# Block 1 of the first sequence: normed by ScalarE, GpSimd and a DMA transpose instead of by matmuls

## The chip, the cores and the metric

The kernel runs on one core of a Trainium2 chip, in one launch. The metric is device time in microseconds (us). The core has five engines, each with its own instruction queue: TensorE (PE, matmuls; its weight loads are shown apart as PEld), VectorE (DVE), ScalarE (ACT), GpSimd (POOL) and SyncE (SP, which only issues DMAs). Matmuls write to PSUM, from where ACT or DVE must copy results to SBUF.

## The reference

Eight sequences of 3008 tokens with 256 channels are mixed along time by a learned filter in the frequency domain, and every token then goes through a gated feed-forward layer of width 1536.

```
X = rfft(x, axis=1);  y = irfft(X * (filt_r + 1j * filt_i), n=3008, axis=1)
t = y.reshape(8 * 3008, 256)
xn = t / sqrt(mean(t * t, axis=-1) + 1e-6) * rms_g
out = (silu(xn @ w_gate) * (xn @ w_val)) @ w_out
```

Inputs and output are float32.

## The kernel before, in words

**The transform.** 3008 = 47 x 64, so the transforms are done in two steps each by matmuls with constant tables. The A-step (`a_unit`, psum tile `psa`) goes over the 64 part, its result is stored to a DRAM scratch `z_tmp` (`z_store`) and read back in another order (`t2_load`); the B-step (`b_unit`, `psb`) goes over the 47 part, and DVE and GpSimd multiply by the filter; DMA transposes (`yt_load`) turn the product; the inverse B-step (`bi_unit`, `psi`) collects in `uu`; four DMA transposes (`t4_load`, tiles `t4`) turn that; the last inverse step is the psum tile `psn` of the norm steps. The first sequence has its own faster variants, written out ahead of the main loop.

**The items.** The feed-forward part of a sequence is cut into 6 blocks (m) of 4 x 128 tokens. A block goes through 12 column groups (jt) of the hidden layer. An item is one (sequence b, block m, group jt): `gv` does four matmuls into `pg` and `pv` (L546; weights `wg` and `wv`, moving operand `xn`), a Silu on ACT (L550) and a product on DVE (L551, tile `hh`); `down`, two items later, does four matmuls with `hh` into `po` (L563). There are 8 x 6 x 12 = 576 items, in that order. So `xn` of block m of sequence 0 is first read by item 12 m.

**What is placed between the items.** Everything else is put into slots by a planner: `at(slot, fn, ...)` appends a step to the plan of an item, and the step is issued between that item's `gv` and its `down`. `fit(slot, need...)` moves a step on to the next slot where the resources that it needs are free: psum bank M (number 0), psum bank B (number 3), and ACT and DVE, whose loads in slots are summed and compared with a room per slot. What is planned first takes its slots first. Steps in the list `late` (`q_unit` alone) come behind `down`.

**How a block is normed.** The usual way (`norm_plan`) has these steps:

- `n_unit`, twice: one matmul of 128x512 into `psn` (L314), copied to the float32 tile `y` by ACT (L195)
- `sq_unit`, twice, an item later: ACT squares two token groups of 256 channels each and sums along the channels (L322, `junk`, sums in `ss`)
- `stat_unit`: GpSimd makes `rho` = (ss / 256 + eps)^-0.5 (L330, L332)
- `xt_unit`: GpSimd multiplies `y` by `rho` into the float16 tile `xt` (L340)
- `tr_unit`: SyncE issues a DMA transpose from `xt` to `xn` (L349), since the matmuls of `gv` need channels on partitions

Block 0 of sequence 0 is done ahead of the loop by `first_norm`. Block 1 of sequence 0 has a way of its own, in which the transform gives `y` already turned, so that no DMA is in it:

- `n_first` in slot 3: eight matmuls of 128x128 (L483) into two psum banks, ACT squares both (L486, `sq`) and copies both to `y`
- `q_unit` in slot 5: eight matmuls of one column with a vector of ones (L497, `psq`) sum the squares; DVE scales (L501), GpSimd takes the power (L503)
- `scale_split` in slot 7: DVE splits `rho` into two float16 parts `hl` (L509, L510)
- `scale_apply` in slot 9: eight matmuls of 128x128 (L519, `psr`) spread `hl` over the partitions, and DVE multiplies (L524) into `xn`

**Queues.** Each engine runs its instructions in the order in which they are issued. SyncE's queue holds the `t4` transposes, the z stores and loads, the xn and yt transposes and the output stores (L581). GpSimd issues the loads of x (`x_load`, L186, 384 KB each, float32 to float16) between its own computations; an x load of the next sequence but one can go once the A-step has read the tile that it overwrites (`xp` has four buffers). Around the change, the first thirteen items of the loop also hold the A-steps 2 to 11 of sequence 1, their four z stores, and the x loads of sequence 2:

```
at(s, a_unit, b, i, e, 0 if k == 'M' else 3)
if i % 3 == 2:
    at(s + 1, z_store, b, i // 3)
    if b + 1 < B:
        at(max(s + 2, XAT.get(b + 1, (0,) * 4)[i // 3]), x_load, b + 1, i // 3)
```

Of the kernel before, what the change touches and what calls it, by code (L numbers as in the profile page):

```python
# [10 lines left out]
FP32 = mybir.dt.float32  # L11
FP16 = mybir.dt.float16
AXT = mybir.ActivationFunctionType
ALU = mybir.AluOpType
# [6 lines left out]
P = 128  # L21
D = 256
B = 8
# [9 lines left out]
Y_SCALE = N * S_INV_B * S_INV_A  # L33
XC = 6
# [67 lines left out]
def kernel(  # L102
# [11 lines left out]
    nc = tc.nc  # L114
# [17 lines left out]
    xtp = ctx.enter_context(tc.tile_pool(name="xtp", bufs=2))  # L132
    up = ctx.enter_context(tc.tile_pool(name="up", bufs=2))
    xnp = ctx.enter_context(tc.tile_pool(name="xnp", bufs=4))
    hp = ctx.enter_context(tc.tile_pool(name="hp", bufs=4))
    op = ctx.enter_context(tc.tile_pool(name="op", bufs=2))
# [4 lines left out]
    psB = ctx.enter_context(tc.tile_pool(name="psB", bufs=1, space=bass.MemoryType.PSUM))  # L141

    tab = glob.tile([P, 5 * P], FP16)
    wa, wai, ident = (tab[:, ts(i, P)] for i in range(3))
# [13 lines left out]
    ones = glob.tile([P, 1], FP16)  # L158
    epsb = glob.tile([P, 1], FP32)
    warm = glob.tile([P, 4], FP32)  # L160
    mhalf = glob.tile([P, 4], FP32)
    seen = glob.tile([P, 4], FP16)

    st = {b: {"x": {}, "t1": {}, "t2": {}, "s": {}, "yt": {}, "t4": {}, "y": {}, "sq": {},
              "u": {}, "xn": {}} for b in range(B)}
# [4 lines left out]
    def y_tile():  # L170
        t = stg.tile([P, 2, 4, 256], FP32, tag="stg", name="y")
        return t.rearrange("p a b c -> p (a b c)")[:, 0:1024].rearrange("p (a e) -> p a e", a=2)
# [16 lines left out]
    def bank(i, name):  # L189
        pool, tag = ((psM, "mx"), (psG, "pg"), (psV, "pv"), (psB, "mb"), (psO, "po0"))[i]  # L190
        return pool.tile([P, 512], FP32, tag=tag, name=name)

    def copy(eng, out, in_, scale=None):
        if eng == "A":
            nc.scalar.activation(out=out, in_=in_, func=AXT.Copy, **({} if scale is None else {"scale": scale}))  # L195
        elif scale is None:
            nc.vector.tensor_copy(out=out, in_=in_)
        else:
            nc.vector.tensor_scalar(out=out, in0=in_, scalar1=scale, scalar2=None, op0=ALU.mult)
# [271 lines left out]
        fill(3)  # L471
        st[0]["xn"][0] = xn

    def n_first(m):
        y = y_tile()
        sq = xtp.tile([P, 4, D], FP16, tag="xt", name="sq").rearrange("p (a e) d -> p a (e d)", a=2)
        psn = [bank((0, 3)[h], "psn") for h in range(2)]
        for h in range(2):
            for q in (2 * h, 2 * h + 1):
                n1p = 4 * m + q  # L480
                src = st[0]["t4"][n1p // XC][:, n1p % XC]
                for dh in range(2):
                    nc.tensor.matmul(psn[h][:, ts(2 * (q % 2) + dh, P)], src[:, ds(dh * P, P)], wai,  # L483
                                     start=True, stop=True)
        for h in range(2):
            nc.scalar.activation(out=sq[:, h, :], in_=psn[h], func=AXT.Square)  # L486
        for h in range(2):
            copy("A", y[:, h, :], psn[h])
        st[0]["sq"][m] = sq
        st[0]["y"][m] = y  # L490

    def q_unit(m):
        sq = st[0]["sq"].pop(m)
        ps = psB.tile([P, 4], FP32, tag="mb", name="psq")
        for q in range(4):
            for dh in range(2):
                nc.tensor.matmul(ps[:, q:q + 1], sq[:, q // 2, ts(2 * (q % 2) + dh, P)], ones,  # L497
                                 start=(dh == 0), stop=(dh == 1))
        u = up.tile([P, 4], FP32, tag="u", name="u")
        rho = up.tile([P, 4], FP32, tag="rho", name="rho")  # L500
        nc.vector.tensor_scalar(out=u, in0=ps, scalar1=1.0 / D, scalar2=1e-6 * Y_SCALE * Y_SCALE,  # L501
                                op0=ALU.mult, op1=ALU.add)
        nc.gpsimd.tensor_tensor(out=rho, in0=u, in1=mhalf, op=ALU.pow)  # L503
        st[0]["u"][m] = rho

    def scale_split(m):
        rho = st[0]["u"].pop(m)
        hl = up.tile([P, 2, 4], FP16, tag="hl", name="hl")
        nc.vector.tensor_copy(out=hl[:, 0, :], in_=rho)  # L509
        nc.vector.tensor_tensor(out=hl[:, 1, :], in0=rho, in1=hl[:, 0, :], op=ALU.subtract)  # L510
        st[0]["u"][m] = hl

    def scale_apply(m, bk):
        hl = st[0]["u"].pop(m)
        y = st[0]["y"].pop(m)
        ps = bank(bk, "psr")
        for q in range(4):
            for e in range(2):
                nc.tensor.matmul(ps[:, ts(q, P)], hl[:, e, q:q + 1].to_broadcast([P, P]), ident,  # L519
                                 start=(e == 0), stop=(e == 1))  # L520
        xn = xnp.tile([P, 4, 2, P], FP16, tag="xn", name="xn")
        pv = ps.rearrange("p (q t) -> p q t", q=4)
        for h in range(2):
            nc.vector.tensor_tensor(out=xn[:, 2 * h:2 * h + 2],  # L524
                                    in0=pv[:, 2 * h:2 * h + 2].unsqueeze(2).to_broadcast([P, 2, 2, P]),
                                    in1=y[:, h, :].rearrange("p (q e t) -> p q e t", q=2, e=2), op=ALU.mult)
        st[0]["xn"][m] = xn

    SPLIT = ((0, 0, 0), (B - 1, 5, JT - 1))
    hh_of = {}  # L530
    po_of = {}
# [78 lines left out]
    with tc.manual_schedule():  # L610
# [48 lines left out]
        todo = [(i, f, dh) for i in range(2) for f in range(2) for dh in range(2)][:7] + [(2, 0, 0)]  # L659
# [56 lines left out]
        first_norm()  # L716

        items = [(b, m, jt) for b in range(B) for m in range(6) for jt in range(JT)]
        plan, late = {}, {}
        front = (sq_unit, s_part, add_unit)  # L720
        load = {r: [0.0] * (len(items) + 99) for r in "MBAV"}
        room = {"A": 0.8, "V": 0.7}
# [2 lines left out]
            load["V"][i] = 0.68  # L725

        def at(slot, fn, *a):
            todo = (late if fn == q_unit else plan).setdefault(slot, [])
            if fn in front:
                todo.insert(0, (fn, a))  # L730
            else:
                todo.append((fn, a))

        def fit(slot, *need, keep=True):
            def fits(r, d, cost):
                i = slot + d
                if r in "MB":
                    return load[r][i] == 0
                wait = 0.0
                for k in range(max(0, i - 16), i + 16):  # L740
                    wait = max(0.0, wait + load[r][k] + (cost if k == i else 0.0) - room[r] - 0.15 * (k < 72))
                    if k >= i and wait > 0.6:
                        return False
                return True

            while not all(fits(*n) for n in need):
                slot += 1
            if keep:
                for r, d, cost in need:
                    load[r][slot + d] += cost  # L750
            return slot

        def norm_plan(b, m, slots, r):
            for i in range(2):
                s = fit(slots[i], ("M", 0, 1), ("A", 0, 0.6), ("A", 1, 0.82))
                at(s, n_unit, b, m, i)
                at(s + 1, sq_unit, b, m, i)
            for d, fn in zip(r, (stat_unit, xt_unit, tr_unit)):
                at(s + d, fn, b, m)
            assert s + r[-1] + 1 < 72 * b + 12 * m  # L760
# [18 lines left out]
        def b_plan(b, slots, lags, soft=()):  # L779
# [18 lines left out]
                        at(last, bi_unit, b, u)  # L798
            return last

        at(3, n_first, 1)
        at(5, q_unit, 1)
        at(7, scale_split, 1)
        at(9, scale_apply, 1, 3)
        load["M"][3] = load["M"][4] = 1
        load["B"][3] = load["B"][4] = load["B"][5] = load["B"][9] = load["B"][10] = 1
        load["A"][3] = load["A"][4] = 1.2
        for m, n_at in ((2, 12), (3, 20), (4, 31), (5, 42)):
            norm_plan(0, m, (n_at, n_at + 2), (2, 3, 6))
        for b in range(1, B):  # L810
            t = (b - 1) * 72
# [31 lines left out]
        early = {}  # L843
# [11 lines left out]
        for i in range(len(items) + 4):  # L855
            for fn, a in early.pop(i, ()):
                fn(*a)
            if i < len(items):
                gv(*items[i])
            for fn, a in plan.pop(i, ()):  # L860
                fn(*a)
            if 2 <= i < len(items) + 2:
                b, m, jt = items[i - 2]
                if jt == 1 and i > JT:
                    down(b, m, 0)
                if jt or i < JT:
                    down(b, m, jt)
                if items[i - 2][2] == JT - 1:
                    stores[i + 1] = items[i - 2][:2]
            for fn, a in late.pop(i, ()):  # L870
                fn(*a)
            if i in stores:
                o_store(*stores[i])
        assert not plan and not late and not early


# [28 lines left out]
```

## Time and profile before

| what | value |
|---|---|
| median of 3 runs | 860.96 us (860.88 to 861.07) |
| the profiled execution's own time | 861.07 us |
| its span, first to last instruction | 859.3 us |
| mean granted TensorE clock | 0.999 |
| busy: PE, PEld | 849.6, 532.8 us |
| busy: DVE, ACT, POOL | 557.2, 612.7, 298.1 us |
| items 0 to 12 start | 43.5 to 61.83 us from the span's start |

The profile is of one execution. Its times count from the first instruction, so they are set against the span, and 1.8 us of the 861.07 lie around it. Busy time is that of an engine's own instructions; matmuls are pipelined, and a matmul's recorded duration is longer than the distance to the next one's start. A timeline row gives the start, the time from the first start to the last end, the engine, the line, the operation with its tiles and the count, and in brackets the idle time before it and what ended that. A DMA's row is only its issue; its landing is in the DMA view, whose packet counts are given by queue: q0 is GpSimd's, q1 SyncE's.

### The profile page before, as it was taken

The page shows a single profiled execution, that of the slowest core. Times are in us where ns is not written, and L with a number is a line of the kernel's source. Part 1 is how long each engine was busy: PE and PEld are TensorE (multiplying, and loading weights), DVE is VectorE, ACT ScalarE, POOL GpSimd, SP SyncE. Part 2 cuts the span into 40 slices and gives each one's busy share as a digit, 9 for nine tenths or more (in the row PEclk, how much of TensorE's full clock was granted, in tenths as well). Part 3 has the DMA queues.
Part 4 walks back from the last instruction along what each step waited for, and adds up shares of the span by engine and source line. Part 5 has one row for each costly group of instructions (what it writes and reads, how often), then busy time and mean ns, then how long its engine had stood idle before and what let it go on. Part 6 is the DMA issues. An engine that isn't in the chain of part 4 may idle for free.

```text
span 859.3 us, 17024 instructions
## 1 busy us (share of the span) xinstructions
PE 849.6 (99%) x6142; PEld 532.8 (62%) x6142; DVE 557.2 (65%) x926; ACT 612.7 (71%) x1339; POOL 298.1 (35%) x346
## 2 busy tenths in 40 slices
PE   8999999999999999999999999999999999999997
PEld 6756666666666666666666666666666666665664
DVE  5857755776666666666666676767666665555554
ACT  4987787787687757887578865887567765777443
POOL 5724832443154412543044430444123430132000
PEclk9999999999999999999999999999999999999999
DMA  9996777755976466756745658434564331521101
GB/s 284 269 202 128 154 157 178 148 123 132 187 137 144 104 145 111 161 117 129 150 121 118 119 107 185 105 81 114 128 118 93 98 72 41 127 49 50 63 25 50
DMA packets 198237, 107.98 MB, mean 126 GB/s; under 512 B 158566, under 2 KB 182520, under 8 KB 198152
## 3 DMA queue, kind: packets, MB, share of 16 engines
q1 hardware_dynamic: 189464, 85.52, 44.4%
q0 software_dynamic: 8544, 21.24, 12.8%
q8 instruction: 48, 0.79, 0.4%
q14 instruction: 37, 0.30, 0.1%
q10 hardware_dynamic: 144, 0.13, 0.0%
HBM read 45.78 MB, written 35.65 MB: 95 GB/s over the span
## 4 chain that ended last, share of the span: by engine, by line
PE 97%; DMA 1%; ACT 1%; DVE 0%; POOL 0%; issue 0%; POOLq 0%
PE po L563 29%; PE pv L546 28%; PE pg L546 28%; PE psb L241 3%; PE psi L285 3%; PE psn L314 2%; PE psa L206 2%; DMA fs<-in_filt_i_dram 1%; PE psy L418 1%; PE psf L389 1%; PE pst L367 0%; POOL xc L186 0%; DVE s L231 0%; ACT ff L195 0%; ACT L470 0%
## 5 line engine op out<-in xcount | busy, mean ns | idle before, releaser
L551 DVE TENSOR_TENSOR hh<-pv,sg 128x512 f16<-128x512 f32 (+2 forms) x578 | 391.8, 678 | 284.1 <-ACT sg L550 222.6
L550 ACT ACTIVATE sg<-pg 128x512 f16<-128x512 f32 (+2 forms) x578 | 337.6, 584 | 215.4 <-PE pg L546 211.5
L546 PE MATMUL pg<-xn,wg 128*128 128x512 f16 (+2 forms) x1156 | 337.9, 374 | 0.1
L546 PE MATMUL pv<-xn,wv 128*128 128x512 f16 (+2 forms) x1156 | 337.8, 374 | 0.0
L563 PE MATMUL po<-wo,hh 128*128 128x256 f16 x2256 | 332.7, 272 | 0.0
L563 PEld LDWEIGHTS <-hh 128*128 128x128 f16 x2256 | 213.5, 98 | 105.1
L268 POOL TENSOR_TENSOR ss<-s,s 128x384 f16<-128x384 f16 x112 | 102.0, 912 | 267.4 <-DVE s L234 239.5
L546 PEld LDWEIGHTS <-wv 128*128 128x128 f16 x1156 | 113.0, 98 | 130.6
L546 PEld LDWEIGHTS <-wg 128*128 128x128 f16 x1156 | 111.5, 98 | 17.0 <-issue 0.3
L340 POOL TENSOR_TENSOR xt<-y,rho 128x1024 f16<-128x1024 f32 (+1 forms) x46 | 85.4, 1857 | 2.9
L322 ACT ACTIVATE junk<-y 128x256 f16<-128x256 f32 x180 | 74.3, 413 | 2.8
L231 DVE TENSOR_TENSOR s<-psb,ff 128x384 f16<-128x384 f32 x124 | 67.7, 548 | 0.7 <-ACT ff L195 0.6
L234 DVE TENSOR_TENSOR s<-psb,ff 128x384 f16<-128x384 f32 x124 | 67.7, 548 | 0.0
L195 ACT ACTIVATE uu<-psi 128x384 f16<-128x384 f32 (+1 forms) x127 | 61.8, 487 | 1.3 <-PE psb L241 0.3
L195 ACT ACTIVATE y<-psn 128x512 f32<-128x512 f32 (+1 forms) x95 | 55.7, 588 | 4.2
L285 PEld LDWEIGHTS <-yt 96*128 96x128 f16 x512 | 35.5, 97 | 26.2 <-issue 0.2
L332 POOL TENSOR_TENSOR rho<-u,mhalf 128x4 f32<-128x4 f32 (+1 forms) x46 | 46.5, 1011 | 3.8
L330 POOL TENSOR_SCALAR u<-ss 128x4 f32<-128x4 f32 (+1 forms) x46 | 8.9, 194 | 106.4 <-ACT junk L322 105.4
L195 ACT ACTIVATE t<-psa 128x512 f16<-128x512 f32 x70 | 41.4, 595 | 2.8 <-PE psa L206 1.4
L285 PE MATMUL psi<-wi,yt 96*128 96x96 f16 x512 | 42.9, 205 | 0.0
L241 PE MATMUL psb<-wb,t 96*128 96x96 f16 x480 | 40.0, 206 | 0.0
L241 PEld LDWEIGHTS <-t 96*128 96x128 f16 x480 | 29.3, 97 | 10.7 <-issue 0.2
(101 smaller groups left out, 364.9 us busy)
## 6 DMA issues: line engine op xcount, KB each, us to landing
out_dram<-o SPq DMA_DIRECT2D x40, 512.0 KB, 3.5
xc<-in_x_dram POOLq DMA_DIRECT2D x31, 384.0 KB, 5.9
z_tmp<-t SPq DMA_DIRECT2D x28, 384.0 KB, 2.7
t<-z_tmp SPq DMA_DIRECT2D x28, 384.0 KB, 5.9
out_dram<-o SPq DMA_DIRECT2D x7, 384.0 KB, 2.7
fs<-in_filt_i_dram POOLq DMA_DIRECT2D x3, 512.0 KB, 10.9
fs<-in_filt_r_dram POOLq DMA_DIRECT2D x3, 512.0 KB, 11.1
ws<-in_moe_w_gate_dram POOLq DMA_DIRECT2D x3, 512.0 KB, 9.8
```

The costliest lines, as they stand in the source:

```text
L195: nc.scalar.activation(out=out, in_=in_, func=AXT.Copy, **({} if scale is None else {"scale": scale}))
L231: eng.tensor_tensor(out=o, in0=ps, in1=f1, op=ALU.mult)
L234: eng.tensor_tensor(out=o, in0=ps[:, :, ::-1, :], in1=f2, op=ALU.mult)
L241: nc.tensor.matmul(ps[:, ts(k, KR)], st[b]["t2"][kk // KC][:, kk % KC, ds(dh * P, P)], wb[0:KR, kk, :], start=True, stop=True)
L268: nc.gpsimd.tensor_tensor(out=ss3[g % 3][:, :, dh, 0:KR], in0=s[0], in1=s[1], op=ALU.add)
L285: nc.tensor.matmul(ps[:, k, :], yt[0:KR, k, dh, :], wi[0:KR, 4 * g + k, :], start=True, stop=True)
L322: nc.scalar.activation(out=junk, in_=y[:, i, ts(u, D)], func=AXT.Square, accum_out=ss[:, 2 * i + u:2 * i + u + 1])
L340: nc.gpsimd.tensor_tensor(out=xt[:, 0:n, :], in0=y.rearrange("p a (u d) -> p (a u) d", u=2)[:, 0:n, :], in1=rho[:, 0:n].unsqueeze(2).to_br ...
L546: nc.tensor.matmul(ps[:, 0:w], wt[:, dt_, ts(jt, P)], xn[:, q0:q1, dt_, :], start=(dt_ == 0), stop=(dt_ == 1))
L550: nc.scalar.activation(out=sg[:, c], in_=pg[:, 0:w], func=AXT.Silu)
L551: nc.vector.tensor_tensor(out=hh[:, c], in0=pv[:, 0:w], in1=sg[:, c], op=ALU.mult)
L563: nc.tensor.matmul(po[s4 // 2][:, s4 % 2, :], hh[:, ts(s4, P)], wo[:, jt, :], start=(jt == 0 and s4 % 2 == 0), stop=(jt == JT - 1 and (s4 ...
```

## The change

The four functions `n_first`, `q_unit`, `scale_split` and `scale_apply` go, and so does the list `late`. Block 1 of sequence 0 is planned by `norm_plan` like blocks 2 to 5, with the wished slots 2 and 3 for the two matmuls, and with the statistics 2, the scaling 3 and the transpose 5 items behind the second matmul. As the block no longer holds the M and B banks by hand, the A-steps of sequence 1, planned later, may find other slots. Behind item 9 every engine has the same order of instructions as before.

```diff
-    def n_first(m):
-        ...
-    def q_unit(m):
-        ...
-    def scale_split(m):
-        ...
-    def scale_apply(m, bk):
-        ...
         items = [(b, m, jt) for b in range(B) for m in range(6) for jt in range(JT)]
-        plan, late = {}, {}
+        plan = {}
...
         def at(slot, fn, *a):
-            todo = (late if fn == q_unit else plan).setdefault(slot, [])
+            todo = plan.setdefault(slot, [])
...
-        at(3, n_first, 1)
-        at(5, q_unit, 1)
-        at(7, scale_split, 1)
-        at(9, scale_apply, 1, 3)
-        load["M"][3] = load["M"][4] = 1
-        load["B"][3] = load["B"][4] = load["B"][5] = load["B"][9] = load["B"][10] = 1
-        load["A"][3] = load["A"][4] = 1.2
+        norm_plan(0, 1, (2, 3), (2, 3, 5))
         for m, n_at in ((2, 12), (3, 20), (4, 31), (5, 42)):
             norm_plan(0, m, (n_at, n_at + 2), (2, 3, 6))
...
-            for fn, a in late.pop(i, ()):
-                fn(*a)
             if i in stores:
                 o_store(*stores[i])
```

## The prediction

> **What bounds the kernel now.** I read the page first: busy time by engine and the chain that ended last.
>
> ```profile
> PE 849.6 (99%) x6142; PEld 532.8 (62%) x6142; DVE 557.2 (65%) x926; ACT 612.7 (71%) x1339; POOL 298.1 (35%) x346
> PE 97%; DMA 1%; ACT 1%; DVE 0%; POOL 0%; issue 0%; POOLq 0%
> ```
>
> TensorE (PE) is busy all the time and carries 97% of the chain. So two things count: how much matmul time the change takes away, and whether it makes PE wait where it never waited. Next I read PE's timeline from 43 us on. Columns: start, duration, operation, count.
>
> ```profile
> 47.96 0.61 PE L483 MATMUL psn<-tab,t 128*128 128x128 f16 x8
> 48.40 0.60 PE L563 MATMUL po<-wo,hh 128*128 128x256 f16 x4
> ...
> 51.66 0.34 PE L497 MATMUL psq<-ones,sq 128*128 128x1 f16 x8
> 51.86 0.59 PE L546 MATMUL pg<-xn,wg 128*128 128x512 f16 x2
> ...
> 57.70 0.61 PE L519 MATMUL psr<-tab,hl 128*128 128x128 f16 x8
> 58.15 0.38 PE L206 MATMUL psa<-xc,tab 128*128 128x512 f16 x1
> ...
> 61.83 0.59 PE L546 MATMUL pg<-xn,wg 128*128 128x512 f16 x2
> 62.26 0.59 PE L546 MATMUL pv<-xn,wv 128*128 128x512 f16 x2
> 62.69 0.38 PE L314 MATMUL psn<-t,tab 128*128 128x512 f16 x1
> 62.91 0.60 PE L563 MATMUL po<-wo,hh 128*128 128x256 f16 x4
> ```
>
> A step costs PE the distance from its start to the next start. 61.83 is the first matmul of item 12, the first that reads block 1's normed xn. Last came the new path's pieces, as block 2 runs them (GpSimd's and SyncE's timelines):
>
> ```profile
> 53.49 1.23 POOL L186 DMA_DIRECT2D xc<-in_x_dram  x2
> 56.87 0.59 POOL L186 DMA_DIRECT2D xc<-in_x_dram  x1 [2.14 <-PE psa L206]
> 68.49 0.19 POOL L330 TENSOR_SCALAR u<-ss 128x4 f32<-128x4 f32 x1 [11.03 <-ACT junk L322]
> 68.78 1.04 POOL L332 TENSOR_TENSOR rho<-u,mhalf 128x4 f32<-128x4 f32 x1
> 69.89 1.89 POOL L340 TENSOR_TENSOR xt<-y,rho 128x1024 f16<-128x1024 f32 x1
> ```
> ```profile
> 71.81 1.26 SPq L349 DMA_TRANSPOSE xn<-xt  x1
> ```
>
> **Matmul time.** Removed: 47.96 to 48.40 (0.44), 51.66 to 51.86 (0.20), 57.70 to 58.15 (0.45): 1.09 us. Added: two psn matmuls of 0.22 (62.69 to 62.91): 0.44. PE gains 0.65 us, and nothing hides it. If that were all, item 12 would start at 61.18.
>
> **The added matmuls' inputs.** They come after items 2 and 3 (46.44 and 48.18). They read the first two t4 transposes; `seen` on GpSimd, released by the second, ran at 46.17, so both are there: no cost. In the built order, three A-step copies change engine or item, and from item 8 on PE's sequence is the old one without psr. DVE loses about 1.8 us (two xn products of 0.68, three small ones), ACT swaps two squares of 0.54 for four. Both have room: from 49 to 53 us ACT was busy 3.53 of 4.00 and DVE 1.41. I cost this at nothing; were a PSUM copy late, PE would lose 0.1 to 0.3 us.
>
> **When is the new xn ready?** ACT sees a matmul 0.42 us after its start (46.44 to 46.86), so the first y copy runs at 46.86 and the second at 48.60. ACT starts one instruction every 0.48 us, a square with its sum every 0.53: two squares from 49.1, item 4's Silu at 50.1, two squares from 50.6, done at 51.6. From block 2's rows, u to the transpose's issue is 71.81 - 68.49 = 3.32. So the transpose is issued at 54.9. Unhindered, such transposes land 3.1 to 3.7 us after issue: 58.6, 2.6 us early.
>
> **But it isn't unhindered.** GpSimd issues in order, and in the built program three x loads of 384 KB stand right behind block 1's xt: those at 53.49, 54.09 and 56.87. The first two now go out at 54.9 and 55.5, together with the transpose; the third needs a matmul that ran by 56.6 and follows at about 56.4. What does a transpose do beside a load? At 388 us the trace has one load and one transpose issued at the same moment (DMA view of 388 to 389.5 us; last number: us to landing):
>
> ```profile
> xc<-in_x_dram POOLq DMA_DIRECT2D x1, 384.0 KB, 5.3
> xn<-xt SPq DMA_TRANSPOSE x1, 6.1
> ```
>
> The packet counts by queue (q0 the loads, q1 SyncE's) from 390.5 to 392 us:
>
> ```profile
> q0 software_dynamic: 78, 0.24, 84.9%
> q1 hardware_dynamic: 74, 0.02, 9.6%
> ```
>
> and, the load over, from 392.5 to 393.5:
>
> ```profile
> q1 hardware_dynamic: 790, 0.20, 114.5%
> ```
>
> The queues take turns one for one: 78 load pieces of 3 KB against 74 transpose pieces of 256 B. A load piece takes 0.849 x 16 x 1.5 / 78 = 0.26 us of an engine, a transpose piece 0.03; alone it takes 1 x 16 / 790 = 0.02. The transpose has 64 pieces per engine, a load 8. So it crawls until no load is queued, then runs out in a rush. The same sum for 388: 25 load pieces had gone by 390.5 (2.3 us after issue, 1.6 per engine); 6.4 x 0.29 = 1.9; the other 58 transpose pieces 1.2; 393.6, landed 394.3: 0.7 more.
>
> For the change: 54.9 + 2.3 = 57.2; three loads are 24 pieces per engine, 22.4 x 0.29 = 6.5, to 63.7; by then 22 of 64 transpose pieces have gone; 42 x 0.02 = 0.84, and 0.7 to land: 65.2. Ends: 61.0 (as beside one load, 6.1) and 67.7 (before's three loads, the last landing 11.9 us after the first's issue, plus 0.9). I take 65.2, as one-for-one turns are what the rows show.
>
> **Sum.** Item 12 waits from 61.18 to 65.2, 4.0 us, and all behind it on PE (the down matmuls of item 10 and on). Net +3.4 us. The profiled run took 861.07 (span 859.3), so 864.5; against the median of 860.96, 864.4. Nothing gives the time back, as PE is full to the end. The z stores queued behind the transpose on SyncE are issued on time (it takes 1.26 us), but their data goes later. Their reader is the t2 load, issued at 66.93 and landing at 71.53 for a matmul at 72.22; that has only 0.7 us of slack, but PE's own delay covers it. The x loads, 1.4 us later, feed A-steps whose first z store is issued at 114.
>
> [...]
>
> **Rivals.**
> First: the transpose is in time, the only effect being the removed matmuls: 860.3. It needs a landing by 61.18, 6.3 us after issue. [...] For it: four transposes beside one load landed in 6.1 to 7.0. Against: one with a second load queued took 7.6 (117.5 to 119 us), and here two more follow.
> Second: it gets through in gaps between loads. From 58 to 59 us in the trace a z store moved 121 pieces against the loads' 20, with two loads queued; 0.9 us alone is 45 transpose pieces. Two such gaps land it between 61.2 and 63.5: 860.3 to 862.6.
> Third, worse than the forecast: the wait halves PE's clock. The windows view shows the gate after the last matmul, which ended at 854.46 (columns: stretch, busy time of PE, PEld, DVE, ACT and POOL, clock, DMA share, GB/s):
>
> ```profile
> 857.80:859.20 1.40, 0.00 (x0) 0.00 (x0) 0.00 (x0) 0.00 (x0) 0.00 (x0) 0.50 0.00 0
> ```
>
> Clock 0.50 some 3.3 us after work ended. A 4.0 us wait is just beyond it; 3.4 us at half clock cost 1.7 more: 866.1. It decides from a wait of some 3.3 us on.
> [...]
> Fourth: the change not doing what it says is excluded by the built order, which has the new steps and lacks the old.
>
> **Chances.** Forecast 0.53, clock halved as well 0.15, gaps 0.14, in time 0.16, and 0.02 for a gain that I don't see. About 0.2% (1.7 us, below 859.2 or above 862.7) is what a measurement of this kernel can tell from no change: slower 0.70, same 0.28, faster 0.02. The range leaves out the in-time case and the upper part of the clock case: 860.9 to 866.3.
>
> **What would show it.** Right: one PE idle stretch of about 4 us just before item 12's first pg matmul, released by the xn DMA; the block-1 transpose landing some 10 us after its issue near 54.9; psn in 0.44 us, no psq or psr. Wrong: a landing before 61.2 and PE without a gap (first rival); a shorter gap (second); clock rows below 1.00 between 65 and 70 us (third); PE waiting at items 2 to 7 instead, which no step here has.

## The result: 865.62 us, slower by half a per cent

| | before | after |
|---|---|---|
| median of 6 runs | 860.98 us (860.88 to 861.12) | 865.62 us (863.66 to 866.87) |
| profiled execution, its span | 861.07, 859.3 us | 865.22, 863.5 us |

The ratio is 1.0053, with a 95% interval of 1.0042 to 1.0063. Forecast were 864.4 us and a range of 860.9 to 866.3. The size is near, but two of its terms were off in opposite directions.

From the page of the changed kernel: PE's busy time, the chain by engine, and the costliest line's group of gate matmuls with its idle time.

```profile
PE 851.5 (99%) x6120; PEld 532.5 (62%) x6120; DVE 557.0 (65%) x923; ACT 612.5 (71%) x1343; POOL 300.2 (35%) x348
PE 95%; DMA 2%; ACT 1%; POOL 1%; DVE 0%; issue 0%; POOLq 0%
L491 PE MATMUL pg<-xn,wg 128*128 128x512 f16 (+2 forms) x1156 | 338.5, 374 | 3.4 <-DMA xn<-xt 3.3
```

PE has 22 instructions fewer and yet 1.9 us more busy time; one wait of 3.3 us for an xn transpose has appeared, and the chain has left PE by 2%. PE's timeline shows where.

```profile
47.99 0.38 PE L314 MATMUL psn<-t,tab 128*128 128x512 f16 x1
48.20 0.60 PE L508 MATMUL po<-wo,hh 128*128 128x256 f16 x4
...
60.55 0.60 PE L508 MATMUL po<-wo,hh 128*128 128x256 f16 x4
64.43 1.01 PE L491 MATMUL pg<-xn,wg 128*128 128x512 f16 x2 [3.29 <-DMA xn<-xt]
65.24 1.06 PE L491 MATMUL pv<-xn,wv 128*128 128x512 f16 x2
...
67.37 0.80 PE L491 MATMUL pg<-xn,wg 128*128 128x512 f16 x2
68.01 0.59 PE L491 MATMUL pv<-xn,wv 128*128 128x512 f16 x2
```

The new psn step costs 0.21 us. Behind the last down step (0.43), item 12 would have started at 60.55 + 0.43 = 60.98 and started at 64.43: 3.45 us. Then the steps themselves are slow: from 64.43 to 68.01 are 3.58 us for what takes 0.86 + 0.22 + 0.43 + 0.43 = 1.94 elsewhere: two gate and two value matmuls, the psn and the down step, and two gate matmuls. The windows view says why (columns as in the prediction: stretch, busy PE, PEld, DVE, ACT, POOL, clock, DMA share, GB/s):

```profile
61.00:64.40 3.40, 0.15 (x2) 0.00 (x0) 0.42 (x1) 0.34 (x1) 0.00 (x0) 0.99 1.07 239
64.40:67.70 3.30, 3.27 (x10) 1.43 (x10) 0.69 (x1) 1.19 (x2) 0.00 (x0) 0.50 0.46 175
67.80:71.00 3.20, 3.20 (x19) 1.73 (x18) 1.55 (x3) 2.76 (x8) 0.00 (x0) 1.00 0.00 0
```

The clock is 0.50 for one stretch of 3.41 us right behind the wait and full again after it: 1.64 us more. The whole account of this execution: matmul time -0.65, wait +3.45, clock +1.64, and -0.19 because its start-up was that much shorter (item 0 at 43.34 instead of 43.53). That is 4.25 us; the spans differ by 4.2.

Why the transpose was late: GpSimd's timeline and then SyncE's.

```profile
51.45 0.19 POOL L330 TENSOR_SCALAR u<-ss 128x4 f32<-128x4 f32 x1 [3.85 <-ACT junk L322]
...
54.70 1.28 POOL L186 DMA_DIRECT2D xc<-in_x_dram  x2
56.46 0.59 POOL L186 DMA_DIRECT2D xc<-in_x_dram  x1 [0.48 <-PE psa L206]
```
```profile
54.78 1.24 SPq L349 DMA_TRANSPOSE xn<-xt  x1
```

The transpose is issued at 54.78, between the first load (54.70) and the two others (about 55.3 and 56.46). Packet counts by queue (q0 the loads, q1 SyncE's), from 57 to 59 us:

```profile
q0 software_dynamic: 108, 0.33, 88.9%
q1 hardware_dynamic: 99, 0.03, 9.4%
```

and from 59 to 60 us:

```profile
q1 hardware_dynamic: 712, 0.18, 86.3%
q0 software_dynamic: 40, 0.08, 39.4%
```

First the turns one for one that the prediction took from the trace of before, 108 against 99. Then, as the first load ends (it lands at 59.7), comes an interval in which 712 of the transpose's 1024 pieces run through in one microsecond, though two more loads had been issued. The rest crawls again beside them, at 65 to 67 pieces in each of the next three microseconds, and the transpose lands at 64.4, 9.6 us after its issue.

### The profile page after: what moved, and what is told of

It is laid out like the page before. It is cut to its first block, busy times and chain, and to the rows that moved or that the text cites. A ratio compares the mean times of both kernels' runs of the same rounds, so it can differ in the third digit from the quotient of the medians.

```text
span 863.5 us, 16987 instructions
## 1 busy us (share of the span) xinstructions
PE 851.5 (99%) x6120; PEld 532.5 (62%) x6120; DVE 557.0 (65%) x923; ACT 612.5 (71%) x1343; POOL 300.2 (35%) x348
## 4 chain that ended last, share of the span: by engine, by line
PE 95%; DMA 2%; ACT 1%; POOL 1%; DVE 0%; issue 0%; POOLq 0%
PE po L508 28%; PE pg L491 28%; PE pv L491 28%; PE psb L241 3%; PE psi L285 3%; PE psn L314 2%; PE psa L206 2%; DMA xn<-xt 1%; DMA fs<-in_filt_i_dram 1%; PE psy L418 1%; PE psf L389 1%; PE pst L367 0%; POOL xc L186 0%; POOL xt L340 0%; DVE s L231 0%
## 5 line engine op out<-in xcount | busy, mean ns | idle before, releaser
L340 POOL TENSOR_TENSOR xt<-y,rho 128x1024 f16<-128x1024 f32 (+1 forms) x47 | 87.3, 1858 | 2.9
```

What stands on the lines that cost most here:

```text
L340: nc.gpsimd.tensor_tensor(out=xt[:, 0:n, :], in0=y.rearrange("p a (u d) -> p (a u) d", u=2)[:, 0:n, :], in1=rho[:, 0:n].unsqueeze(2).to_br ...
```

## The experiments

The theory: the cost is the transpose caught between three x loads, plus the clock that its wait brings down; the matmul part of the change is a gain of 0.65 us. The rivals: the transpose is slow by itself; the loads matter by their place elsewhere; the wait alone, or the clock alone, makes up the loss. "Gate" below is this line behind block 1's `norm_plan`, a GpSimd copy of a piece of the new xn into a scratch tile. The copy reads what the transpose writes, and the loads that stand behind it in GpSimd's program are to go out only when it is done:

```diff
+        at(9, lambda: nc.gpsimd.tensor_copy(out=seen, in_=st[0]["xn"][1][:, 0, 0, 0:4]))
```

**two_loads, one_load, loads_held: two, one and none of the three loads beside the transpose.** All have the gate; two_loads has nothing else.

```diff
-        XAT = {2: (6, 8, 11, 29), ...
+        XAT = {2: (6, 10, 11, 29), ...     one_load
+        XAT = {2: (10, 10, 11, 29), ...    loads_held
```

> Two x loads go out with the transpose, the third waits until it has landed. Theory: the transpose moves some 800 pieces until the second load's pieces start near 59.7, crawls beside its 8 pieces per engine (8 x 0.29 = 2.3 us) and ends behind it: landing 62.3 to 63.0, PE waits 1.4 to 2.0 us, too short to halve the clock: 861.7 to 862.4 us. Rival (the third load alone does the harm): landing below 61 and 860.3. Rival (the path itself): 863.7 or more.

> One x load goes out with the transpose, the two others wait until it has landed. Theory: 6.1 to 6.4 us from issue to landing, 60.9 to 61.2 us against a need at 61.0: PE waits 0 to 0.3 us, 860.3 to 860.6 us. Rival (the path itself): as in the changed kernel, 863.7 or more. Rival (a load costs the transpose nothing unless several are queued): landing below 59, and 860.3.

> All three x loads wait on GpSimd until block 1's transpose has landed (a copy of four columns of xn ahead of them). Theory (transpose and loads take turns one for one on each DMA engine): the transpose, issued near 54.8 us, lands alone after 3.1 to 3.7 us, at 58 to 58.5; item 12 does not wait; PE keeps the 0.65 us of removed matmuls: 860.3 us. Rival (the new path itself is slow: squares, GpSimd, or the z stores ahead of it on SyncE's queue): it lands near 64 as in the changed kernel, and the time stays at 863.7 or more.

| kernel | median, us (range, runs) | ratio (95%) |
|---|---|---|
| two_loads | 862.80 (862.47 to 864.75, 7) | 1.0027 (1.0016 to 1.0038) |
| one_load | 861.99 (861.47 to 865.11, 10) | 1.0015 (1.0006 to 1.0025) |
| loads_held | 862.00 (861.64 to 864.00, 10) | 1.0012 (1.0002 to 1.0021) |

The wait list of PE from 40 to 80 us, its largest entry, for two_loads:

```profile
PE pg L491 <- DMA xn<-xt: 2.3, 1, 2.3
```

for one_load:

```profile
PE psb L241 <- DMA t<-z_tmp: 2.0, 1, 2.0
```

and for loads_held:

```profile
PE psb L241 <- DMA t<-z_tmp: 2.1, 1, 2.1
```

Two loads beside the transpose leave 2.3 of the 3.3 us of wait; with one or none the wait at item 12 is gone. The gate copy, which waits for the landing, ran at 63.49, 61.07 and 57.76, that is 8.7, 6.0 and 3.1 us after the transpose's issue, and the next load went out behind it, at 64.01, 61.59 and 58.25. So it is not slow by itself, and each load beside it costs. The landings came near what was expected, but none of the three medians did. two_loads missed by 0.4 us. one_load and loads_held missed by more and are still 1 us above before, as the wait has moved to the first psb, the reader of the t2 load. In loads_held the three loads now go out from 58.25 on and meet the last z store, issued at 61.26: it lands at 69.50, so the t2 load can only be issued at 69.64 and lands at 73.51. In one_load the z store is in time, but the t2 load itself runs beside two late loads and takes from 66.34 to 73.78. Those are the 0.7 us of slack that the prediction had seen and thought covered by PE's own delay: the cover was the delay at item 12, and it went with it.

The slowest loads_held execution, 864.0, is the profiled one, and it shows something about the clock:

```profile
71.35:74.70 3.35, 1.22 (x12) 0.86 (x12) 1.45 (x3) 0.28 (x1) 0.00 (x0) 1.00 1.21 247
74.80:78.10 3.30, 3.30 (x11) 1.51 (x10) 0.85 (x2) 1.60 (x3) 0.91 (x1) 0.50 0.85 143
```

A wait of only 2.1 us (71.43 to 73.56) halved the clock here. The traces show at which times the clock changes. In the changed kernel it drops at 64.36, is back at 67.77, 3.41 us later, and drops again at 863.08, behind the last matmul. In loads_held it drops at 74.76 and at 859.82. In steps of 0.02 us the windows view puts the half clock of the changed kernel at 3.413 us. The distances between the drops, 798.72 and 785.06 us, are 234 and 230 times that. From these two executions comes an estimate: the clock changes at edges 3.413 us apart, and the drop behind the last matmul tells where they lie in an execution. In loads_held the wait lay whole inside the 3.41 us ahead of the drop (71.34 to 74.76), and PE was idle for 62% of them (2.13 of 3.41). In one_load (last drop at 858.24) the estimate has an edge at 73.17, which cuts the wait of 2.0 us in two, and in two_loads (860.92) one at 62.20, which cuts the wait of 2.3 us. In both the clock stayed full. (Three of two_loads' seven runs took 864.28 to 864.75 us at a mean clock of 0.998 or 0.996; the edge may lie otherwise there, but no trace shows it.)

**fill_wait: the clock alone.** Fourteen matmuls whose result nobody reads stand ahead of item 12, so PE is not idle while it waits.

```diff
             ...
+            if i == JT:
+                fill(14, 3)
```

> The changed kernel with 14 matmuls without use (3.0 us) in front of item 12, so that PE has little idle time in its wait; nothing else differs. Theory (the wait costs 3.4 us, the rest of the loss is PE at half clock behind it): clock 1.00 throughout, 863.6 to 863.9 us, all runs within 0.5 us. Rival (the rest of the loss and the spread of 863.7 to 866.9 come from when the transpose lands): median near 865.6 and a spread of 2 us or more.

Measured: 864.49 (863.80 to 865.25, 4 runs), ratio 1.0040 (1.0025 to 1.0055). This is neither the theory's 863.6 to 863.9 nor the rival's 865.6. The mean clock is 1.000 in all four runs. In the changed kernel it is 0.998 or 0.996 in five of the six, and the sixth, at 1.000, took 863.66, at least 1.6 us less than the five. (A mean of 0.998 alone proves nothing: one run of the kernel before has it too, at 860.85 us.) So the wait and the clock both cost time. But the 1.1 us between the two medians are not the price of the clock, since the transpose need not land at the same time in both. In the profiled execution the fill ended at 64.19 and PE still waited until 66.04:

```profile
64.40:67.70 3.30, 1.66 (x10) 0.97 (x10) 0.40 (x1) 0.93 (x2) 0.00 (x0) 1.00 0.53 189
67.80:71.10 3.30, 3.30 (x20) 1.80 (x19) 1.86 (x4) 3.05 (x10) 0.00 (x0) 1.00 0.00 2
```

The landing was thus 1.6 us later than in the changed kernel's profile, with all issues within 0.03 us of it. That is as much as the clock had cost there, so it is chance that the two profiled executions took the same time, 865.25 and 865.22 us. The interval behind the first load was where it had been: from 59 to 60 us SyncE's queue moved 740 pieces here, and 712 there. What differed was how long the pieces that were left took, and why is not shown. As to the clock, what was left of the wait, 1.85 us or at most 54% of any 3.41 us, did not halve it: 1.00 in both rows.

**spread_a, spread_b: the loads moved away from the transpose, the last z store and the t2 load.** Both have the gate.

```diff
-        XAT = {2: (6, 8, 11, 29), ...
+        XAT = {2: (4, 10, 23, 29), ...    spread_a
+        XAT = {2: (10, 23, 26, 29), ...   spread_b
```

> The x loads of sequence 2 are spread: the first goes out ahead of block 1's statistics (47.6 us), the second after the transpose has landed, the third behind the first products of block 2 (about 77 us). Theory (the transposes take turns with loads, and held loads only pushed the last z store and so the t2 load late): the transpose lands by 59, the last z store by 65.5, the t2 load in time, no wait on PE: 860.3 us, 0.6 below before. Rival (the t2 load is late because of the transpose itself, not of the loads): PE waits some 2 us before the first psb as with all loads held, 862.0. Rival (the early load delays the z store ahead of the transpose): landing after 61, 860.5 to 861.5.

> The first x load waits until block 1's transpose has landed (58 us), the second and third go out behind the first products of block 2 (about 77 and 83 us). Theory: transpose down by 58.3, last z store issued at 61.3 behind one load only, landing by 64.5; no wait of PE in either place: 860.3 us. Rival (the t2 load is late because of the transpose): wait before the first psb, 862.0. Rival (the moved loads now slow the yt transposes from 78 us on and PE waits there): 860.5 to 862.

Measured: spread_a 860.30 (860.09 to 860.87, 11 runs), ratio 0.9993 (0.9984 to 1.0002); spread_b 860.30 (median of 12; all but one from 860.08 to 860.65), ratio 0.9991 (0.9982 to 1.0001). The one spread_b execution that stands apart, 868.04, is the profiled one. It has no wait near item 12, but two later ones, near 97 and 100 us:

```profile
PE psi L285 <- DMA yt<-ss: 2.5, 1, 2.5
PE pg L491 <- DMA xn<-xt: 2.4, 1, 2.4
```

Two x loads went out there at 87.11 and 91.52, and the xn transpose issued at 86.83 landed 12.2 us later. In spread_a, whose next load went out at 90.77, the same transpose took 4.3. So the last rival of spread_b, that the moved loads slow transposes elsewhere, came true in this one of the twelve runs.

In spread_a the load that was moved ahead went out at 47.17 and landed at 56.9, so it still ran beside the transpose for its first 2 us. The gate copy ran at 59.01, 4.2 us after the transpose's issue, one load followed at 59.52 and the third only at 77.31. SyncE's timeline shows the t2 load back on time:

```profile
66.98 1.58 SPq L221 DMA_DIRECT2D t<-z_tmp  x3
```

It lands at 71.02, and PE has no wait above 0.2 us from 45 to 80 us. That is the change without its side effects: 0.6 us below the 860.92 of before in the same runs, where the removed matmuls give 0.65. The ranges overlap only between 860.63 and 860.87, but the interval of the ratio still holds 1: a gain of this size is at the edge of what these runs can tell.

**half_pieces: the loads stay where they are, in smaller pieces.** No gate and the slots of the change; each of the three loads is issued as two DMAs of 192 KB, with pieces of 1.5 KB instead of 3.

```diff
-            nc.gpsimd.dma_start(t.rearrange("p a d -> p (a d)"), src(N2, XC))
+            if b == 2 and c < 3:
+                for lo in (0, 3):
+                    nc.gpsimd.dma_start(t[:, lo:lo + 3, :].rearrange("p a d -> p (a d)"), src(N2, 3, lo))
+            else:
+                ...
```

> The changed kernel with each of the three x loads issued as two of half the columns, so that a piece is 1.5 KB instead of 3 KB and a load has twice as many; bytes and order are the same. Theory (the queues take turns piece for piece): the transpose gets twice as many turns in the same time and lands at 61.5 to 62.5, PE waits 0.6 to 1.6 us: 860.9 to 862.0 us. Rival (the queues share by bytes or time): the landing stays near 64.4, 863.6 to 865.6 us.

Measured: 860.65 (860.24 to 861.31, 10 runs), ratio 0.9997 (0.9988 to 1.0006), and no wait at item 12. It beat its own expectation. The packets by queue from 58 to 59 us:

```profile
q1 hardware_dynamic: 851, 0.22, 112.0%
q0 software_dynamic: 27, 0.02, 14.0%
```

With the first half load gone (landed at 58.78), 851 pieces of SyncE's queue ran in this microsecond against 27 of the loads, although GpSimd had issued all six half loads by 58.55 (from 54.79 on). As in the changed kernel at 59 us, the transpose gets its rush when one load ends; here that end comes a microsecond earlier, and what had still to go afterwards was little. So it was this interval that removed the wait, and not the expectation's twice as many turns. The size of a piece and the number of loads changed together, and no run tells which of the two counts.

**spread_only: is the gate needed?** spread_a without its copy on GpSimd, so one line of the change's schedule.

```diff
-        XAT = {2: (6, 8, 11, 29), ...
+        XAT = {2: (4, 10, 23, 29), ...
```

> The changed kernel with the three x loads at slots 4, 10 and 23 and nothing else, so without the copy on GpSimd that spread_a has. Theory (the transpose needs only that no load is queued in the first 4 us or so after its issue; the load of slot 10 is held by its psum and tile dependence on a matmul near 58.8 us anyhow): transpose landed by 59.5, no PE wait at item 12, 860.1 to 860.6. Rival (the copy was needed: without it the slot-10 load goes out beside the transpose): a landing of 60 to 63 us, PE waits up to 2 us, 860.3 to 862.5.

Measured: 862.07 (861.57 to 862.51, 11 runs), ratio 1.0013 (1.0004 to 1.0022). My theory was wrong and the rival right. GpSimd's timeline and PE's wait list:

```profile
46.89 1.22 POOL L186 DMA_DIRECT2D xc<-in_x_dram  x2
...
54.77 0.64 POOL L186 DMA_DIRECT2D xc<-in_x_dram  x1
```
```profile
PE pg L491 <- DMA xn<-xt: 1.2, 1, 1.2
```

The load of slot 10 doesn't wait for a matmul of its own slot: it is free to go at 54.77, right behind xt, as the second load was before. And the load that was moved ahead, issued at 47.4, lands only at 57.40. So the transpose has two loads beside it in turn, and PE waits 1.2 us. All that differs from spread_a is the copy, which there holds the load of slot 10 back until the transpose has landed: 862.1 against 860.3.

**before_spread: does the spread gain anything by itself?** The kernel before with that same line.

> The kernel before with the three x loads spread (slots 4, 10 and 23 instead of 6, 8 and 11), block 1 still normed by matmuls. Theory (the 0.6 us that spread_a and spread_b gained over the kernel before come from the 0.65 us of removed matmul time; the spread of the loads only keeps the new transpose free): no gain here, 860.7 to 861.2 with psn, psq and psr in place and no wait of PE from 45 to 80 us. Rival (the spread itself gains, since it frees the DMA engines for other transfers that PE waits for): 860.2 to 860.5.

Measured: 860.98 (860.82 to 861.16, 11 runs), ratio 1.0001 (0.9992 to 1.0010). No gain, so what spread_a and spread_b are below the kernel before comes with the changed norm, as the matmul time says.

## Why the prediction was right, and where it was not

- **Matmul time**: right. The removed and added steps were to give 0.65 us. From item 0 to item 12 before took 18.30 (43.53 to 61.83); after, without the wait, 17.64 (43.34 to 60.98): 0.66. Spread_a shows it in the time.
- **The added matmuls' inputs**: right; PE has no wait between 45 and 60 us.
- **When is the new xn ready**: right to about 0.1 us. u was forecast at 51.6 and ran at 51.45, and from u to the transpose's issue are 3.33 us (forecast 3.32).
- **But it isn't unhindered**: the mechanism is shown, by three, two, one and no loads beside the transpose, with waits of 3.3, 2.3, none and none. The landing was forecast 10.3 us after issue and took 9.6. The term that was mis-sized is the 22.4 load pieces per engine that the transpose was to wait out in turns of one for one. That holds while a load runs (99 pieces against 108 from 57 to 59 us), but behind the first load there was an interval that carried 712 pieces at once. This is the second rival's mechanism, and it was given too little: the interval stands in the profiles of the changed kernel, of fill_wait and of two_loads (712, 740 and 735 pieces from 59 to 60 us), and in half_pieces it comes earlier and removes the wait.
- **Sum and third rival**: the clock did drop in the profiled run, and by mean clock and time together in four others of the six. The price was right (1.7 forecast, 1.64 measured), the condition wrong. The 3.4 us at half clock behind that price stand in no row of before, whose span ends 1.6 us after its drop (857.70 to 859.3); the changed kernel showed 3.41. "From a wait of some 3.3 us on" came from the one place in the trace of before where PE stopped for good. In loads_held 2.1 us were enough. With that in view, the third rival should have been in the likeliest case and not beside it with 0.15: wherever edges 3.413 us apart lie (the estimate above), a wait of 3.45 us covers at least half of some stretch between two of them, and 62% of one, as in loads_held, in about three positions of four. By the prediction's own signs, clock rows below 1.00 between 65 and 70 us, it is the third rival that came, with the second's shorter wait. The wait was 0.6 us shorter than forecast, and the clock cost 1.64 where the sum had nothing. So 864.4 is only 1.2 below the median because the two errors partly cancel, and that the range holds the result is in part luck.
- **The t2 load's slack**: the sentence that PE's own delay covers it holds for the changed kernel, where psb has no wait. It also said what would happen without that delay, and loads_held and one_load show it.
- **First rival**: what the time would be with the transpose on time, 860.3, is what spread_a and spread_b measure; it needed the loads elsewhere, and half_pieces, with smaller loads in the same places, comes near it at 860.65. In the changed kernel itself the transpose landed at 64.4, 3.2 us after the 61.18 that this rival needed.

What stays open: why the loads that are already issued leave an interval of about a microsecond behind the end of the first. The runs show the interval, its place and what it carries, and not its cause. Open too is why the pieces left behind it took longer in fill_wait.

## What to carry to other kernels

Work taken off a full engine and given to a DMA is priced by what is queued beside that DMA at its issue, not by its duration elsewhere: here 3.1 us alone and 9.6 in company. Where a wait is removed by moving transfers, look up the next transfer with little slack first; here it was the t2 load with 0.7 us, and both simple moves of the loads ran into it. And a wait on PE may cost more through the clock: here 3.45 us of wait cost 1.64 us on top, and in loads_held 2.1 us were enough to halve the clock. So price both or see to it that there is no wait.

## What was new of the hardware

- The granted clock fell to 0.50 behind 3.41 us of which PE was idle for 62% (loads_held: a wait of 2.13 us), and it stayed at 1.00 behind fill_wait's wait of 1.85 us, at most 54% of any 3.41 us. In the changed kernel it stayed at 0.50 for 3.41 us. These are single executions, and no run shows how much idle time it takes.
- Between two queued loads on GpSimd's queue, SyncE's queue moved 712 (changed kernel) and 851 pieces (half_pieces) in one microsecond, against about 50 (99 in 57 to 59 us) to 67 (62 to 63 us) per microsecond while a load of whole size ran in the changed kernel.
- Two loads of half the size in place of one, with pieces of 1.5 KB, cost the loads nothing that PE felt and took the whole wait away (half_pieces, no wait of PE above 0.2 us from 40 to 80 us).
